# Linear attention with a gated feed-forward block: fewer turns of the identity at the start, one stored form of x sooner, and the last tile's sum added in PSUM

## The chip, the cores and the metric

The kernel runs on one core of one Trainium2 chip. The metric is the device time of one execution in microseconds. A core has a matrix engine (TensorE, PE in the profile), a vector engine (VectorE, DVE), a scalar engine (ScalarE, ACT), a general engine (GpSimd, POOL) and a queue engine (SyncE, SP), which issues nearly all transfers here. SBUF is the working memory and PSUM the memory that TensorE writes, in eight banks.

## The reference

All arrays are float32: x is 2048 by 576, `wqkv` 576 by 1728, `wo` 576 by 576, `w_gate` and `w_up` 576 by 4608, `w_down` 4608 by 576; there are 32 heads of 18.

```python
xn = layernorm(x)
q, k, v = split(xn @ wqkv)                 # per head
phi = lambda t: where(t > 0, t + 1, exp(t)) + 1e-6
kv  = einsum("sd,se->de", phi(k), v);  z = phi(k).sum(0)
s   = (phi(q) @ kv / (phi(q) @ z + 1e-6)) @ wo
h   = gelu(xn @ w_gate) * (xn @ w_up)
out = x + s * silu(h @ w_down)
```

## The kernel before, in words

Every large product is made of float32r words: an operand is cut into a high word (a ScalarE copy) and a low word (a VectorE subtraction), and several passes of TensorE add up their products in a PSUM bank. The rows of x are sixteen tiles of 128; four tiles make a block of 512 (`TBN`), and pairs of blocks make the two halves `s = 0, 1`. The columns of x are split in two halves j.

All instructions are pinned to the order in which the program writes them, on each engine (`keep_in_program_order`), so the listing is the schedule. `big(i, ...)`, `mid(i, ...)` name SBUF slots with one buffer each: a tile made in a slot waits until all users of the tile before it there are done. `bank` takes one of six PSUM banks in turn, `own_bank` one of two others.

**The start.** TensorE turns (transposes) a 128 by 128 identity into a bank that nobody reads, in the loop at L1230, while the first loads arrive. Then tile 0 of x is normalized (`spread`, `scales`, `center` on VectorE, with two small steps on ScalarE), transposed by `turn(0)` (L205), copied out by `save` on ScalarE, and multiplied by the raw weights (`x_mm_plain`). For the tiles after it, `turn`, `place` (the words of x, named xo_B), `save` and `x_mm` (L128, tile kv) repeat; the words of the weights are made by `kv_hi` on ScalarE and `kv_lo` on VectorE or GpSimd (tile wkv).

**Between the two halves.** After tile 7 the q products of blocks 0 and 1 run, five groups each, through `q_store(tb, gi)`: TensorE fills a bank, ScalarE and VectorE form phi of it (tiles e_q and ph), GpSimd adds the two, and SP stores the result. Group 4 is a group of mixed rows that are only transposed. The dictionary `behind` says what is written behind each group. `form(nm)` cuts one of four differences of blocks of x (T1, T3, T2, T4, made by `difference`) into words in slot 12 and stores it in DRAM: one copy of 1536 columns on ScalarE, two subtractions on VectorE, and one transfer on SP of 1280 KB (tile xo_T, stored as kept_T). Tiles 8 and 9 of x are prepared in the same stretch (`turn(N0)`, `place(N0)`, `center(N0 + 1)`, `spread(N0 + 2, 2)`), and then the kv tiles of the second half begin. `spread_sel` and what follows turn kv and q into s.

**The feed-forward block.** Gate and up run as products of block matrices with sums of blocks formed beforehand (`matrix`, L769), and h goes to DRAM in pieces (hs). The down product takes 26 products (`PROD`), each of nine K-tiles (`kt`), in four banks of 288 columns, one for each row tile j; `read` adds banks into the accumulators (`acc`). `UNITS` says which K-tiles go together: 0 to 3 in the first two units, 4 to 8 in the rest.

**The end.** In the last product `down_all` leaves the loop after the first two units, closes the output of the product before, and then runs K-tiles 4 to 8 tile by tile (j = 0 to 3). Behind each tile `close_last` adds the bank to the accumulator on VectorE and takes Silu on ScalarE; the multiplication with s, the addition of x and the store (`rest`) are written one tile later. The last tile does all this in two halves of 144 columns.

Of the kernel before, what the change touches and what calls it, by code (L numbers as in the profile page):

```python
# [11 lines left out]
AF = mybir.ActivationFunctionType  # L12
# [10 lines left out]
HALF = D // 2  # L23
# [3 lines left out]
TT = TBN // P  # L27
# [47 lines left out]
PROD = (  # L75
# [8 lines left out]
)  # L84
SIGN = (-1, 1, -1, -1, 1, -1, 1, 1)
# [5 lines left out]
def block_kernel(ctx, tc, x, xe, wq_d, wkv_d, wo, wgu_d, wd_d, out):  # L91
# [9 lines left out]
    def own_bank(name):  # L101
        return ps.tile([P, 512], F32, tag="own", bufs=2, name=name)

    def big(i, shape, dt, name):
        return sb.tile(shape, dt, tag=f"b{i}", bufs=1, name=name)
# [7 lines left out]
    def gl_tile(shape, name, dt=F32):  # L113
        return sb.tile(shape, dt, tag="gl", bufs=6, name=name)
# [6 lines left out]
    def act(*args, **kw):  # L121
        pin(nc.scalar.activation(*args, **kw))  # L122

    def vec(op, *args, **kw):
        pin(getattr(nc.vector, op)(*args, **kw))  # L125
# [7 lines left out]
    def dma(out, in_, eng=None):  # L133
        tc.keep_in_program_order((eng or nc.sync).dma_start(out=out, in_=in_))
# [42 lines left out]
    def scales(n0):  # L177

        n, mv, st = mom.pop(n0)
        v, r, c = (st[:, i, 0:n] for i in range(1, 4))  # L180
        if n == 1:
            vec("tensor_scalar", c, r, r, -0.5, op0=ALU.mult, op1=ALU.mult)
            vec("tensor_scalar", c, c, v, 1.5, op0=ALU.mult, op1=ALU.add)
            vec("tensor_scalar", c, c, r, None, op0=ALU.mult)
        else:
            vec("scalar_tensor_tensor", c, r, -0.5, r, op0=ALU.mult, op1=ALU.mult)
            vec("tensor_mul", c, c, v)
            vec("scalar_tensor_tensor", c, c, 1.5, r, op0=ALU.add, op1=ALU.mult)
        for t in range(n):
            scale_of[n0 + t] = mv[:, t, 0:1], c[:, t : t + 1]  # L190

    def center(n):

        xs = xstat[n // 2][:, n % 2]
        m, r = scale_of.pop(n)
        vec("tensor_scalar", xs, xs, m, r, op0=ALU.subtract, op1=ALU.mult)
# [258 lines left out]
    def q_mm(tb, gi, o):  # L455
        s, b = divmod(tb, 2)
        pq = bank(f"q_{tb}_{gi}")
        if gi == NHG - 1:
            t = qt.pop(tb)
            for i in range(TT):  # L460
                pin(nc.tensor.transpose(
                    pq[:, i * P : (i + 1) * P], t[:, i].rearrange("p r j -> p (r j)"), ident
                ))
        else:
            n = 0
            for j, nm in enumerate(BS[b]):
                for wi, xi, rows in PASSES:
                    mm(
                        pq, q_part(j, wi, slice(gi * P, (gi + 1) * P)), xo[s][nm][:, xi, :],
                        start=(n == 0), stop=(n == 2 * len(PASSES) - 1),  # L470
                    )
                    n += 1
        phi(o, pq, f"q{tb}_{gi}")

    def q_store(tb, gi):
        if tb not in ph_d:
            ph_d[tb] = dr.tile([P, NHG, TBN], F32, name=f"phd_{tb}")
        o = gl_tile([P, TBN], f"ph_{tb}_{gi}")
        q_mm(tb, gi, o)
        dma(out=ph_d[tb][:, gi, :], in_=o)  # L480
# [395 lines left out]
    def run_events(at):  # L876
        for f in events.pop(at, []):
            f()
# [54 lines left out]
    reg, acc_t, banks, raw_v, hi_v, word, early = {}, {}, {}, {}, {}, {}, {}  # L933

    def load_reg(at, nm, third=None):
        if at not in reg:
            b = big(REG[at], [P, REG_W], F32, f"b_{at}")
            reg[at] = b[:, 0 : KT * HALF].rearrange("p (k d) -> p k d", k=KT)
        j, c = int(nm[0]) - 1, int(nm[1]) - 1
        par, f = divmod(KP[j], 2)  # L940
        src = wd_d[par::2, :, f, c * HALF : (c + 1) * HALF].rearrange("g p d -> p g d")
        k = slice(0, KT) if third is None else slice(3 * third, 3 * third + 3)
        dma(out=reg[at][:, k], in_=src[:, k])
# [133 lines left out]
    def acc_of(o):  # L1077
        i, j = ACCS[o]
        if i not in acc_t:
            acc_t[i] = big(i, [P, 2, TT, HALF], F32, f"acc_{i}")  # L1080
        return acc_t[i][:, j]
# [19 lines left out]
    sxs = {}  # L1101

    def places(o):
        i, c = divmod(o, 2)
        tb = TP[i]
        cols = slice(c * HALF, (c + 1) * HALF)
        rows = lambda j: slice(tb * TBN + j * P, tb * TBN + (j + 1) * P)
        return tb, cols, rows
# [22 lines left out]
        vec("tensor_add", t[:, 0], t[:, 0], t[:, 1])  # L1131
        stores.append(lambda: dma(out=out[rows(j), cols], in_=t[:, 0]))

    def close_last(o, j, p, parts):

        _, cols, rows = places(o)
        w = HALF // parts
        y, t, b = acc_of(o)[:, j], sxs[o][j], banks[p % 2][j]
        d = dict(PROD[p][3])[o]
        cs = [slice(i * w, (i + 1) * w) for i in range(parts)]  # L1140
        for c in cs:
            vec("tensor_add" if d > 0 else "tensor_sub", y[:, c], y[:, c], b[:, c])
            act(y[:, c], y[:, c], AF.Silu, scale=float(SIGN[o]))

        def rest():
            for c in cs:
                z = t[:, 0, c]
                vec("tensor_mul", z, y[:, c], z)
                vec("tensor_add", z, z, t[:, 1, c])
                dma(  # L1150
                    out=out[rows(j), cols.start + c.start : cols.start + c.stop], in_=z
                )

        return [rest]

# [17 lines left out]
    def down_all():  # L1173
        late = []
        last = NP - 1
        for u in range(NP * NU):
            p, k = divmod(u, NU)
            n = KT * p + 2 * k
            for at in sorted(events):
                if at <= H_END + n // 2:  # L1180
                    run_events(at)
            if p in LOADS and k < 3:
                load_reg(*LOADS[p], k)
            if k == 0:
                for o, e in ENDS.items():
                    if e == p:
                        load_sx(o)
            if k < 2:
                change(p + 1, k)
                if p in SHARED:  # L1190
                    make_words(p + 1, k)
            elif k < 4:
                make_words(p + 1, k - 2)
                if p + 1 in SHARED and p:
                    make_words(p + 2, k - 2)
            cut(u + 2)
            if p == last and k == 2:
                break
            for kt in range(*UNITS[k]):
                down_mm(p, kt, range(TT))  # L1200
            load_unit(p + 1, k)
            run(stores)
            if k == 1 and p:
                read(p - 1)
                late += [
                    lambda o=o, j=j: close(o, j) for o, e in ENDS.items() if e == p - 1
                    for j in range(TT)
                ]
            else:
                run(late, 2)  # L1210
        run(late)
        run(stores)
        o = next(o for o, e in ENDS.items() if e == last)
        for j in range(TT):
            for kt in range(UNITS[2][0], KT):
                down_mm(last, kt, (j,))
            late += close_last(o, j, last, 2 if j == TT - 1 else 1)
            run(late, len(late) - 1)
        run(late)

# [6 lines left out]
        ins=[], outs=[], act_func_set_id=LN_EXP,  # L1227
    )))
    first = [own_bank(f"idle_{i}") for i in range(2)]
    for i in range(34):  # L1230
        pin(nc.tensor.transpose(first[i % 2][:, 0:P], ident, ident))  # L1231
    load_x(0, 1)
    load_kv(0, 0)
# [86 lines left out]
    for n in range(3, 2 * TT):  # L1320
# [3 lines left out]
        if n >= TT:  # L1324
            j, c = divmod(n - TT, 2)
# [16 lines left out]
    N0 = 2 * TT  # L1342

    def form(nm):
        keep(0, nm, build(0, nm, 12))

    behind = {
        (0, 0): [lambda: kv_mm(N0 - 1), lambda: spread(N0, 2), lambda: difference(0, 3)],
        (0, 1): [lambda: scales(N0), lambda: center(N0), lambda: q_store(1, 4)],
        (0, 2): [lambda: form("T1")],  # L1350
        (0, 3): [lambda: turn(N0), lambda: place(N0)],
        (1, 0): [lambda: form("T3"), lambda: save(N0)],
        (1, 1): [lambda: center(N0 + 1), lambda: spread(N0 + 2, 2), lambda: scales(N0 + 2)],
# [143 lines left out]
```

## Time and profile before

| | |
|---|---|
| median of 3 runs | 1473.43 us (1472.06 to 1473.94) |
| the profiled execution, its own time | 1472.68 us |
| its span | 1470.9 us |
| busy TensorE, VectorE, ScalarE, GpSimd | 1461.8, 1138.0, 572.0, 579.1 us |
| turns of the identity | 34, from 1.75 us to 8.05 us |
| end of TensorE, end of VectorE | about 1465.6 us, 1468.1 us |

In the rows, "out<-in" names the tile that is written and the tiles that are read, with buffer numbers left out. A row of the timeline begins with the start and the length in microseconds; several like instructions are merged ("x4"), and the bracket tells how long the engine was idle before it and what ended that. A line number can be that of a helper: L125 is every VectorE operation, L122 every ScalarE operation, L131 GpSimd's, L128 every plain matmul, L134 every transfer.

### The profile page before, as it was taken

The numbers are of one execution on the slowest core, as the hardware profiler recorded it, in microseconds if no ns is written. First come the engines' busy times: TensorE is split into PE (matmuls) and PEld (weight loads), VectorE is DVE, ScalarE is ACT, GpSimd is POOL, SyncE is SP. The second block draws the span as 40 slices with busy tenths as digits, with TensorE's granted clock in tenths as the row PEclk, the third lists the DMA queues.
The fourth block names the chain that finished last, engine by engine and source line by source line (L and its number), as shares of the span: only waits on it lengthen the run. The fifth ranks groups of instructions, "written<-read, shape, count | busy, mean of one in ns | idle before, by whom it ended". The sixth has DMA issues, their size and how long they took to land.

```text
span 1470.9 us, 21966 instructions
## 1 busy us (share of the span) xinstructions
PE 1461.8 (99%) x8184; PEld 1303.9 (89%) x8184; DVE 1138.0 (77%) x1581; ACT 572.0 (39%) x936; POOL 579.1 (39%) x513
## 2 busy tenths in 40 slices
PE   9999999999999999999999999999999999999998
PEld 8989989988888888888888888888889999999998
DVE  7566477466878788877778888778788978989888
ACT  5445355433222332223223223322335556455444
POOL 3332340125655667655674755757632000000000
PEclk9999999999999999999999999999999999999999
DMA  4435004442242323334153242423379888767886
GB/s 175 157 135 204 5 2 180 147 189 86 93 144 97 125 87 116 128 115 136 51 172 100 94 136 73 157 87 101 128 271 345 270 258 253 244 190 233 278 287 216
DMA packets 116148, 230.43 MB, mean 157 GB/s; under 512 B 10874, under 2 KB 44410, under 8 KB 113994
## 3 DMA queue, kind: packets, MB, share of 16 engines
q1 hardware_dynamic: 113386, 216.97, 44.0%
q0 software_dynamic: 2656, 12.06, 2.2%
q8 instruction: 65, 1.06, 0.3%
q14 instruction: 41, 0.34, 0.1%
HBM read 146.37 MB, written 82.58 MB: 156 GB/s over the span
## 4 chain that ended last, share of the span: by engine, by line
PE 96%; DVE 2%; issue 1%; DMA 0%; ACT 0%; POOL 0%; ACTq 0%; DVEq 0%; POOLq 0%
PE bd L128 23%; PE ga L769 16%; PE al L769 16%; PE de L769 16%; PE kv L128 8%; PE be L769 8%; PE s L128 4%; PE q L128 3%; PE kv_a L128 1%; PE xt L205 1%; DMA raw_h<-hs 0%; PE idle L1231 0%; PE d L128 0%; PE kw L128 0%; DVE acc L125 0%
## 5 line engine op out<-in xcount | busy, mean ns | idle before, releaser
L131 POOL TENSOR_TENSOR sm<-raw 128x384 f32<-128x384 f32 x72 | 75.2, 1044 | 152.0 <-DMA raw<-in_wgu_dram 107.4
L128 PE MATMUL kv<-wkv,xo_B 128*128 128x388 f32 (+2 forms) x658 | 127.9, 349 | 0.5 <-DVE xo_B L125 0.4
L128 PEld LDWEIGHTS kv<-wkv,xo_B 128*128 128x128 f32 x658 | 118.8, 188 | 2.4 <-DVE xo_B L125 0.7
L125 DVE TENSOR_TENSOR wa<-sm,wa 128x768 fp32r<-128x768 f32 x72 | 92.5, 1285 | 36.1 <-ACT wa L122 35.2
L128 PE MATMUL bd<-w_head,hi 128*128 128x288 f32 x516 | 118.0, 294 | 0.0
L125 DVE TENSOR_TENSOR wb<-raw,wb 128x256 fp32r<-128x256 f32 (+1 forms) x108 | 107.0, 991 | 7.3 <-ACT wb L122 5.8
L125 DVE TENSOR_TENSOR wa<-raw,wa 128x256 fp32r<-128x256 f32 x72 | 68.2, 947 | 50.7 <-ACT wa L122 49.6
L122 ACT ACTIVATE hi<-raw_h 128x1024 fp32r<-128x1024 f32 x59 | 62.4, 1059 | 90.0 <-PE bd L128 60.9
L128 PE MATMUL bd<-w_end,hi 128*128 128x288 f32 x448 | 89.8, 294 | 0.0
L122 ACT ACTIVATE spot_h<-spot_h 128x512 f32<-128x512 f32 x49 | 30.8, 633 | 151.4 <-DVE spot_h L125 151.4
L128 PEld LDWEIGHTS bd<-w_head,hi 128*128 128x128 f32 x516 | 87.0, 188 | 0.1
L125 DVE TENSOR_TENSOR raw_h<-raw_h,hi 128x1024 fp32r<-128x1024 f32 x59 | 71.9, 1223 | 16.7 <-ACT hi L122 16.7
L128 PE MATMUL bd<-w_end,raw_h 128*128 128x288 f32 x264 | 77.9, 295 | 0.0
L122 ACT ACTIVATE u<-al 128x512 f32<-128x512 f32 x72 | 41.0, 592 | 90.0 <-PE al L769 60.9
L122 ACT ACTIVATE wa<-sm 128x1152 fp32r<-128x1152 f32 x36 | 41.8, 1161 | 84.8 <-PE de L769 84.8
L128 PEld LDWEIGHTS bd<-w_end,hi 128*128 128x128 f32 x448 | 71.9, 188 | 0.0
L128 PE MATMUL bd<-beside,raw_h 128*128 128x288 f32 x240 | 70.9, 295 | 0.0
L131 POOL TENSOR_TENSOR spot_h<-spot_h,spot_h 128x512 f32<-128x512 f32 x45 | 62.3, 1390 | 2.9 <-DVE spot_h L125 2.4
L769 PE MATMUL ga<-xo_B,wb 128*128 128x512 f32 x252 | 63.0, 389 | 0.0
L769 PE MATMUL al<-xo_B,wa 128*128 128x512 f32 x252 | 63.0, 389 | 0.0
L769 PE MATMUL al<-xr_B,wb 128*128 128x512 f32 x252 | 63.0, 389 | 0.0
L769 PE MATMUL al<-xr_B,wa 128*128 128x512 f32 x252 | 63.0, 389 | 0.0
(261 smaller groups left out, 4066.5 us busy)
## 6 DMA issues: line engine op xcount, KB each, us to landing
raw_h<-hs SPq DMA_DIRECT2D x176, 256.0 KB
raw<-in_wgu_dram SPq DMA_DIRECT2D x36, 768.0 KB
hs<-spot_h SPq DMA_DIRECT2D x90, 256.0 KB
hs<-spot_g SPq DMA_DIRECT2D x80, 256.0 KB
b<-in_wd_dram SPq DMA_DIRECT2D x42, 432.0 KB
hs<-spot_m SPq DMA_DIRECT2D x38, 256.0 KB
raw_g<-hs SPq DMA_DIRECT2D x22, 256.0 KB
kept_T<-xo_T SPq DMA_DIRECT2D x4, 1280.0 KB
```

Source lines behind the costliest of these rows:

```text
L122: pin(nc.scalar.activation(*args, **kw))
L125: pin(getattr(nc.vector, op)(*args, **kw))
L128: pin(nc.tensor.matmul(*args, **kw))
L131: pin(getattr(nc.gpsimd, op)(*args, **kw))
L205: pin(nc.tensor.transpose(xts[n][j][:, k, :], xs[:, j, k * P : (k + 1) * P], ident))
L769: nc.tensor.matmul(o, w[0:rows, wi, :], xop[0:rows, xi, :], start=(start and n == 0), stop=(n == len(PASSES) - 1), skip_group_check=True,)
```

## The change

The loop at the start makes 28 turns for 34. `form("T1")` moves from behind q group 2 of block 0 to behind q group 1, ahead of `q_store(1, 4)`; so T1's ScalarE copy, its two VectorE subtractions and its store on SP now come before the phi and the stores of the mixed group and of q group 2. The order of TensorE's instructions is the same but for the six turns. For the last row tile, a new step `add_in` adds the accumulator into the PSUM bank on VectorE, ahead of the last five K-tiles; these K-tiles then add to it in the bank, Silu reads the bank itself with the sign folded into its scale, and the last tile is closed in one piece of 288 columns, with one store for two.

```diff
+    def add_in(o, j, p):
+
+        b = banks[p % 2][j][:, 0:HALF]
+        vec("tensor_add" if dict(PROD[p][3])[o] > 0 else "tensor_sub", b, b, acc_of(o)[:, j])
+
-    def close_last(o, j, p, parts):
+    def close_last(o, j, p, added):
...
-        for c in cs:
-            vec("tensor_add" if d > 0 else "tensor_sub", y[:, c], y[:, c], b[:, c])
-            act(y[:, c], y[:, c], AF.Silu, scale=float(SIGN[o]))
+        if added:
+            act(y, b, AF.Silu, scale=float(SIGN[o] * d))
+        else:
+            vec("tensor_add" if d > 0 else "tensor_sub", y, y, b)
+            act(y, y, AF.Silu, scale=float(SIGN[o]))
...
         o = next(o for o, e in ENDS.items() if e == last)
+        add_in(o, TT - 1, last)
         for j in range(TT):
             for kt in range(UNITS[2][0], KT):
                 down_mm(last, kt, (j,))
-            late += close_last(o, j, last, 2 if j == TT - 1 else 1)
+            late += close_last(o, j, last, j == TT - 1)
             run(late, len(late) - 1)
...
-    for i in range(34):
+    for i in range(28):
         pin(nc.tensor.transpose(first[i % 2][:, 0:P], ident, ident))
...
-        (0, 1): [lambda: scales(N0), lambda: center(N0), lambda: q_store(1, 4)],
-        (0, 2): [lambda: form("T1")],
+        (0, 1): [
+            lambda: scales(N0), lambda: center(N0), lambda: form("T1"), lambda: q_store(1, 4),
+        ],
```

More of the change, by code (lines that the diff above doesn't have):

```diff
@@ L1132, in close @@
         stores.append(lambda: dma(out=out[rows(j), cols], in_=t[:, 0]))
-    def close_last(o, j, p, parts):
+    def add_in(o, j, p):
+        b = banks[p % 2][j][:, 0:HALF]
+        vec("tensor_add" if dict(PROD[p][3])[o] > 0 else "tensor_sub", b, b, acc_of(o)[:, j])
+    def close_last(o, j, p, added):
         _, cols, rows = places(o)
-        w = HALF // parts
-        y, t, b = acc_of(o)[:, j], sxs[o][j], banks[p % 2][j]
+        y, t, b = acc_of(o)[:, j], sxs[o][j], banks[p % 2][j][:, 0:HALF]
         d = dict(PROD[p][3])[o]
-        cs = [slice(i * w, (i + 1) * w) for i in range(parts)]
-        for c in cs:
-            vec("tensor_add" if d > 0 else "tensor_sub", y[:, c], y[:, c], b[:, c])
-            act(y[:, c], y[:, c], AF.Silu, scale=float(SIGN[o]))
-        def rest():
[L1146 to L1152, printed above, removed]
+        if added:
[3 more added lines that the diff above has]
+            act(y, y, AF.Silu, scale=float(SIGN[o]))
+        def rest():
+            z = t[:, 0]
+            vec("tensor_mul", z, y, z)
+            vec("tensor_add", z, z, t[:, 1])
+            dma(out=out[rows(j), cols], in_=z)
         return [rest]
```

## The prediction

> **What bounds the kernel now.** I read the page first (busy shares, then the chain that ended last), then the waits of TensorE alone, and then the timeline around each of the three places that the change touches.
>
> ```profile
> span 1470.9 us, 21966 instructions
> ...
> PE 1461.8 (99%) x8184; PEld 1303.9 (89%) x8184; DVE 1138.0 (77%) x1581; ACT 572.0 (39%) x936; POOL 579.1 (39%) x513
> ...
> PE 96%; DVE 2%; issue 1%; DMA 0%; ACT 0%; POOL 0%; ACTq 0%; DVEq 0%; POOLq 0%
> ```
>
> TensorE (PE) bounds it. It is idle for 1470.9 - 1461.8 = 9.1 us in all, so nothing that leaves its own work alone can win more than that. The waits of TensorE (total, times, longest) say where the idle time before the tail lies:
>
> ```profile
> PE idle L1231 <- POOL ident masks.py:199: 1.8, 1, 1.8
> PE xt L205 <- issue: 0.5, 1, 0.5
> PE kv L128 <- DVE xo_B L125: 0.4, 1, 0.4
> ...
> PE xt L205 <- DVE x L125: 0.2, 1, 0.2
> ```
>
> Only the 0.4 and the 0.2 belong to the stage that the change re-orders. The other things it can reach are TensorE's own "work" on the identity at the start, and what comes after its last matmul. A microsecond taken from the head or from a wait of TensorE is a microsecond off the end, as long as TensorE stays the bound in between, which it is in 96% of the chain.
>
> **Part 1, 28 turns for 34.** The windows of the tile idle give their pace (columns: PE busy and count, weight loads busy and count):
>
> ```profile
> 1.75:6.50 4.75, 4.75 (x23) 4.75 (x23) 1.00 0.96 350
> 6.50:7.81 1.31, 1.31 (x13) 1.31 (x12) 1.00 0.98 395
> ```
>
> Twenty-two turns fit into the first 4.75 us (one of the 23 straddles the border): 0.216 us each. The last twelve take 1.31 us: 0.109 each. The pace doubles near 6.5 us, while the granted clock reads 1.00 throughout, so the records of the clock do not show this step and the pitch does. Six turns fewer are six of the fast kind, if the step comes at the same time: 6 x 0.109 = 0.65 us. Whether the first transposes of x can use that, and whether it gets through to the end, is read from the chain (start, length, piece) and from VectorE's rows:
>
> ```profile
> 1.75 6.30 PE idle L1231 x34
> 8.05 0.51 PE xt L205 x3
> ...
> 8.58 0.50 ACT xf_B L122
> ...
> 12.94 0.87 ACT xo_B L122 x2
> ...
> 15.01 1.99 POOL wkv L131
> ...
> 18.86 6.83 PE kv L128 x36
> ```
>
> ```profile
> 6.41 0.68 DVE L125 TENSOR_SCALAR x<-x,mv,st 128x768 f32<-128x768 f32 x1
> ...
> 10.58 0.68 DVE L125 TENSOR_SCALAR x<-x,mv,st 128x768 f32<-128x768 f32 x1
> 11.18 1.61 DVE L125 TENSOR_TENSOR wkv<-rw,wkv 128x832 fp32r<-128x832 f32 x2
> 13.46 1.51 DVE L125 TENSOR_TENSOR xo_B<-xt,xo_B 128x256 fp32r<-128x256 f32 x4 [0.67 <-ACT xo_B L122]
> ```
>
> Tile 0 of x is ready at 6.41 + 0.68 = 7.09, and TensorE comes to it only at 8.05, so up to 0.96 can be used; with 28 turns it comes at 7.40, still after x, and the turns still cover the wait. From there the chain hands the shift on: ScalarE's copy waits for the transposes, the plain matmuls for the copy, and the second turn needs tile 1 of x, ready at 11.26, well ahead of 12.58 - 0.65 = 11.93. ScalarE's xo_B and wkv, GpSimd's wkv and the matmuls at 18.86 follow one another. VectorE is the one that could hold it: it is free at 12.79 and waited 0.67 until 13.46, just more than the 0.65 asked for; behind that it follows ScalarE or its own work and moves along. I take 0.65. Bounds: 0 if the pace steps up so early that x is the later one in both kernels, and 6 x 0.216 = 1.3 if it steps up after the turns.
>
> The Trainium skill (TensorE: Matmul & The Clock Gate, "Part 1: The HAM clock gate") says why this length can vary: the clock opens after a busy window of some 3.4 us, the window runs free of the kernel's start, and the warm-up is a time and not a number of matmuls. By it, an estimate: the step falls between one and two windows after the first turn, between 5.2 and 8.6 us here, and the six turns are worth anything between 0 and 1.3 us. The one trace has the step at 6.5, inside that.
>
> **Part 2, the first transformed form (T1) a group of q sooner.** T1, T3 and T2 are cut into the same buffer (slot 12) and each is stored from it, so each waits for the store of the one before. Rows of the timeline, in order of time:
>
> ```profile
> 95.32 0.64 ACT L122 ACTIVATE e_q<-e_q 128x512 f32<-128x512 f32 x1
> ...
> 99.58 1.48 ACT L122 ACTIVATE xo_T<-xf_B 128x1536 fp32r<-128x1536 f32 x1
> ...
> 101.15 2.20 DVE L125 TENSOR_TENSOR xo_T<-xf_B,xo_T 128x1024 fp32r<-128x1024 f32 x2 [1.41 <-ACT xo_T L122]
> ...
> 103.41 0.32 SPq L134 DMA_DIRECT2D kept_T<-xo_T  x1
> ...
> 109.30 1.49 ACT L122 ACTIVATE xo_T<-xf_B 128x1536 fp32r<-128x1536 f32 x1 [2.57 <-DMA kept_T<-xo_T]
> ...
> 112.81 0.32 SPq L134 DMA_DIRECT2D kept_T<-xo_T  x1
> ...
> 118.77 1.48 ACT L122 ACTIVATE xo_T<-xf_B 128x1536 fp32r<-128x1536 f32 x1
> ...
> 123.95 1.51 DVE L125 TENSOR_TENSOR xo_B<-xt,xo_B 128x256 fp32r<-128x256 f32 x4
> ...
> 124.43 2.15 PE L128 MATMUL kv<-wkv,xo_B 128*128 128x416 f32 x10 [0.37 <-DVE xo_B L125]
> ...
> 126.08 0.68 DVE L125 TENSOR_SCALAR x<-x,mv,st 128x768 f32<-128x768 f32 x1
> ...
> 126.82 0.87 PE L205 MATMUL xt<-ident,x 128*128 128x128 f32 x6 [0.24 <-DVE x L125]
> ```
>
> A store takes 109.30 - 103.41 = 5.9 us until ScalarE may go on. After the change T1's ScalarE cut follows the exponential of q group 1, ending 95.96, and runs to 97.4; VectorE's subtractions follow the centring and take 2.20, to about 100.4; the store goes out at 100.4 instead of 103.41, 3.0 us sooner. T3 can then start at 106.3 instead of 109.30; ScalarE has a group's phi in front of it, so I say 106.9. T3's store goes out at about 110.4 and lands at 116.3; T2 starts at 116.4 instead of 118.77, 2.4 us sooner. Behind T2 stand the things that TensorE waits for: xo_B of tile 9 on ScalarE and VectorE (123.95) and the centring of tile 10 (126.08). They come some 2.4 us sooner, and the two waits need only 0.37 and 0.24. Both go: 0.61 us.
>
> What the move delays: on ScalarE and VectorE the phi of the group of mixed rows and of q group 2 wait behind T1, by some 2.2 us; GpSimd's additions to them follow, and on SP T1's store now stands in front of those two phi stores. TensorE needs their PSUM banks only six allocations later, at the groups that it starts at about 105 and 108, when they have been read since about 101.5. ScalarE's phi of q group 3 can slip by 2 us behind GpSimd's addition, which would cost T3 0.2. None of it reaches TensorE, so nothing is charged. Bounds: 0.61, all that TensorE waits there, and 0 if the waits only move on to the next tile.
>
> **Part 3, the last sum.** VectorE's last row of work, TensorE's row for the last tile, and the transfers (window, last two columns DMA share and GB/s):
>
> ```profile
> 1462.29 0.81 DVE L125 TENSOR_TENSOR acc<-acc,bd 128x288 f32<-128x288 f32 x2
> ...
> 1463.42 0.29 PE L128 MATMUL bd<-beside,hi 128*128 128x288 f32 x1
> ...
> 1464.97 0.46 DVE L125 TENSOR_TENSOR sx<-sx 128x288 f32<-128x288 f32 x1
> ...
> 1465.60 0.52 DVE L125 TENSOR_TENSOR acc<-acc,bd 128x144 f32<-128x144 f32 x2 [0.17 <-PE bd L128]
> ...
> 1466.04 0.45 DVE L125 TENSOR_TENSOR sx<-acc,sx 128x288 f32<-128x288 f32 x1
> 1466.52 0.46 DVE L125 TENSOR_TENSOR sx<-sx 128x288 f32<-128x288 f32 x1
> 1466.90 0.30 DVE L125 TENSOR_TENSOR sx<-acc,sx 128x144 f32<-128x144 f32 x1
> ...
> 1467.80 0.31 DVE L125 TENSOR_TENSOR sx<-sx 128x144 f32<-128x144 f32 x1
> ```
>
> ```profile
> 1467.80:1468.40 0.60, 0.00 (x0) 0.00 (x0) 0.30 (x1) 0.00 (x0) 0.00 (x0) 0.50 0.69 246
> 1468.40:1469.40 1.00, 0.00 (x0) 0.00 (x0) 0.00 (x0) 0.00 (x0) 0.00 (x0) 0.50 0.49 148
> ```
>
> Today VectorE stands before 1465.60 until TensorE has ended, with the multiply and the addition of tile 2 queued behind it, and then has eight instructions left, ending at 1468.11. After: the new addition into PSUM runs at 1462.29, before the two of that row, and pushes what follows by 0.36 (the pitch of that row: 0.81 - 0.45). The wait goes; tile 2's multiply follows the row at 1464.97 directly: 1464.97 + 0.36 + 0.38 = 1465.7, tile 3's a pair later (1466.90 - 1466.04 = 0.86) at 1466.6, its addition ends about 1467.5. ScalarE's Silu reads the bank when TensorE ends, about 1465.6; the copy out of PSUM at 8.58 took 0.50 for 384 columns, so 288 end by 1466.1, before 1466.6: VectorE's queue, no longer TensorE, sets it. That is 0.57 sooner. The store is now one of 288 columns, not the second of two halves: tile 2's, of that size, had its last bytes 1468.40 - 1466.98 = 1.4 us after its addition (1466.52 + 0.46), the half 1469.40 - 1468.11 = 1.3. So 0.1 goes back; I take 0.44, between 0 and 0.6.
>
> The new wait: TensorE's tile 3 needs the addition, done at 1462.74, and starts at 1463.42. The cover is 0.68 us; without it each microsecond is one at the end, and nothing but tile 3's fifteen matmuls is queued there.
>
> **Sum.** 0.65 + 0.61 + 0.44 = 1.70 us. The profiled execution took 1472.68 us, 1.78 around its span; it gives 1470.98. It lies 0.75 below the median of the three runs, 1473.43, to which the measured time answers: 1473.43 - 1.70 = 1471.7.
>
> **The rivals.**
> - The pace steps up early and x is late anyway: part 1 is worth nothing, 1.05 stays, 1472.4. For it: x is only 0.31 earlier than the new end of the turns. Against: this trace. 0.10.
> - The pace steps up late: 1.3 for part 1, 2.35 in all, 1471.1. 0.12.
> - The two waits of part 2 only move on, and the change does not do there what it says: 1.09, 1472.3. Against: 2.4 us of lead for 0.61. 0.08.
> - The new addition comes late and TensorE waits in front of tile 3: it decides from 0.68 us of delay of VectorE, which has eight instructions waiting for loads and Silus before it; at 1.5 us late part 3 is a loss of 0.4 and the time 1472.6. 0.07.
> - Slower: fewer turns are too little to lift the pace. They then all run at 0.216, 28 x 0.216 = 6.05, and end where they end now; part 1 is gone, and the matmuls after them run at half pace for as long as the first stretch lasted, 4.75 us, which loses 2.4. Net 1.05 - 2.4: 1.3 slower, 1474.8; two such stretches 1477.1. It decides if a gap such as the one before the plain matmuls falls where the turns used to be. Against: the pace rose near 6.5, before the new end at 7.4. 0.08.
> - The forecast: 0.55, alone 1470.4 to 1473.0.
>
> **How the numbers follow.** The three runs before lie between 1472.06 and 1473.94, and a measurement of this kernel can tell about 0.2%, 2.9 us, from no change. Faster by more than that, below 1470.5, needs the late step and a kind scatter: 0.07 from the forecast, 0.06 from the second rival, 0.13. Slower by more needs the two slow stretches, or a longer wait than priced: 0.06. The rest, 0.81, is within it. The range takes in the first four rivals and the scatter of the runs: 1470.2 to 1473.9.
>
> **What would show it.** Right: idle ends near 7.4 and transposes of x begin there; the matmuls now at 18.86 begin near 18.2; T1's store is issued near 99.8 and T2's cut starts near 115.7 (both less 0.65); neither wait of 0.37 and 0.24 is left; VectorE's last addition ends some 1.9 us after TensorE instead of 2.5. Wrong: turns at 0.216 to their end, a wait of kv or xt of like size a tile later, a wait of bd for VectorE before the last fifteen matmuls, or a last store that takes longer than 1.4 us.

## The result, and the profile after

| | before | after |
|---|---|---|
| median | 1472.54 us (1471.28 to 1473.94, 19 runs) | 1470.32 us (1469.58 to 1471.74, 19 runs) |
| the profiled execution, its span | 1472.68, 1470.9 us | 1470.93, 1468.6 us |

The ratio is 0.9985, with a 95% interval of 0.9979 to 0.9992: 2.2 us less, 0.15%. Forecast were 1.7 us less, and no change larger than 0.2%.

The page of the kernel after, the same lines as before:

```profile
span 1468.6 us, 21945 instructions
...
PE 1459.7 (99%) x8178; PEld 1302.2 (89%) x8178; DVE 1134.3 (77%) x1578; ACT 571.9 (39%) x935; POOL 579.0 (39%) x513
...
PE 95%; DVE 2%; issue 1%; ACT 1%; DMA 1%; POOL 0%; SPq 0%; DVEq 0%; ACTq 0%; POOLq 0%
```

TensorE still bounds it. Its busy time fell by 2.1 us, 1.7 of it in the turns (4.62 us, by the windows below, for 6.30). The waits of TensorE after (total, times, longest), without the one before the first turn (1.8) and one of 0.2 in tile b, which both kernels have:

```profile
PE xt L205 <- PE idle L1234: 1.0, 1, 1.0
PE xt L205 <- issue: 0.6, 1, 0.6
PE kv L128 <- ACT xf_B L122: 0.3, 1, 0.3
PE ga L769 <- DVE u L125: 0.2, 1, 0.2
```

The 0.4 for xo_B and the 0.2 for x are gone, as forecast. New is the first row: 1.0 us in which TensorE has no turns left and x is not there yet. It carries the name of the turns, but it ends when x comes, as the next rows show.

**The start.** The turns by windows (PE busy and count, then weight loads), the head of the chain of waits, and VectorE's row for tile 0 of x, all after:

```profile
1.75:4.25 2.50, 2.50 (x12) 2.50 (x13) 1.00 0.91 307
4.25:4.75 0.50, 0.50 (x5) 0.50 (x4) 1.00 1.09 449
4.75:6.50 1.75, 1.62 (x15) 1.38 (x13) 1.00 1.01 402
```

```profile
1.75 4.63 PE idle L1234 x28
6.38 0.97 issue
7.36 0.53 PE xt L205 x3
...
8.46 3.45 PE kv L128 x8
...
18.20 6.82 PE kv L128 x36
```

```profile
6.58 0.68 DVE L125 TENSOR_SCALAR x<-x,mv,st 128x768 f32<-128x768 f32 x1
```

The pace rose at about 4.4 us, not at 6.5: 2.50/12 = 0.21 us a turn before it, 1.62/15 = 0.11 behind it. The turns ended at 6.38, a microsecond ahead of the forecast; x was ready at 6.58 + 0.68 = 7.26 and the transposes began at 7.36. The 36 matmuls at 18.86 now begin at 18.20, 0.66 sooner.

**The transformed forms.** Rows picked from the timeline after: ScalarE's cuts of T1, T3, T2 and the stores of the first two, then tile 9's words, tile 10's centring, and TensorE's rows beside them:

```profile
95.27 1.47 ACT L122 ACTIVATE xo_T<-xf_B 128x1536 fp32r<-128x1536 f32 x1
99.58 0.32 SPq L134 DMA_DIRECT2D kept_T<-xo_T  x1
106.03 1.48 ACT L122 ACTIVATE xo_T<-xf_B 128x1536 fp32r<-128x1536 f32 x1
109.53 0.32 SPq L134 DMA_DIRECT2D kept_T<-xo_T  x1
115.50 1.47 ACT L122 ACTIVATE xo_T<-xf_B 128x1536 fp32r<-128x1536 f32 x1
117.33 8.00 PE L128 MATMUL kv<-wkv,xo_B 128*128 128x412 f32 x42
120.67 1.51 DVE L125 TENSOR_TENSOR xo_B<-xt,xo_B 128x256 fp32r<-128x256 f32 x4
122.80 0.68 DVE L125 TENSOR_SCALAR x<-x,mv,st 128x768 f32<-128x768 f32 x1
125.17 0.82 PE L205 MATMUL xt<-ident,x 128*128 128x128 f32 x6
```

T3's cut no longer waits for T1's store (no bracket at 106.03). Tile 10 of x is ready at 123.48, 1.7 us ahead of its transposes at 125.17. TensorE goes through its 42 matmuls without a gap: 125.17 - 117.33 = 7.84 us. The row of before that answers to it:

```profile
117.94 6.13 PE L128 MATMUL kv<-wkv,xo_B 128*128 128x412 f32 x32
```

There the same stretch takes 126.82 - 117.94 = 8.88. I call this length T below; the move made it 1.04 us shorter, not 0.61.

**The end.** Rows picked from the timeline after: the addition into the bank, tile 3's first and last matmul, Silu out of the bank, and VectorE's last two; then the last matmul of before.

```profile
1460.40 0.46 DVE L125 TENSOR_TENSOR bd<-bd,acc 128x288 f32<-128x288 f32 x1
1461.74 0.29 PE L128 MATMUL bd<-beside,hi 128*128 128x288 f32 x1
1463.59 0.29 PE L128 MATMUL bd<-w_end,raw_g 128*128 128x288 f32 x1
1463.92 0.41 ACT L122 ACTIVATE acc<-bd 128x288 f32<-128x288 f32 x1 [0.41 <-PE bd L128]
1464.67 0.45 DVE L125 TENSOR_TENSOR sx<-acc,sx 128x288 f32<-128x288 f32 x1
1465.16 0.46 DVE L125 TENSOR_TENSOR sx<-sx 128x288 f32<-128x288 f32 x1
```

```profile
1465.27 0.29 PE L128 MATMUL bd<-w_end,raw_g 128*128 128x288 f32 x1
```

VectorE ends 1465.62 - 1463.88 = 1.74 us after TensorE, where it took 1468.11 - 1465.56 = 2.55. From TensorE's end to the end of the span it is 4.72, and was 5.34: 0.62 less.

So the span's 2.3 us are 0.66 + 1.04 + 0.62. Between these places the gate and up stage is 0.5 longer in this pair and the down stage 0.5 shorter, in code that the change does not touch.

### The profile page after: what moved, and what is told of

It reads as the page before. It is cut to its first block, busy times and chain, and to the rows that moved or that the text cites. A ratio compares the mean times of both kernels' runs of the same rounds, so it can differ in the third digit from the quotient of the medians.

```text
span 1468.6 us, 21945 instructions
## 1 busy us (share of the span) xinstructions
PE 1459.7 (99%) x8178; PEld 1302.2 (89%) x8178; DVE 1134.3 (77%) x1578; ACT 571.9 (39%) x935; POOL 579.0 (39%) x513
## 4 chain that ended last, share of the span: by engine, by line
PE 95%; DVE 2%; issue 1%; ACT 1%; DMA 1%; POOL 0%; SPq 0%; DVEq 0%; ACTq 0%; POOLq 0%
PE bd L128 24%; PE ga L769 15%; PE de L769 15%; PE al L769 15%; PE kv L128 8%; PE be L769 8%; PE s L128 4%; PE q L128 3%; PE kv_a L128 1%; PE xt L205 1%; DVE sx L125 1%; DMA hs<-spot_h 1%; DVE wb L125 0%; PE d L128 0%; PE kw L128 0%
## 5 line engine op out<-in xcount | busy, mean ns | idle before, releaser
L769 PE MATMUL ga<-xr_B,wb 128*128 128x512 f32 x252 | 63.0, 389 | 0.0
```

The source lines that it names most:

```text
L769: nc.tensor.matmul(o, w[0:rows, wi, :], xop[0:rows, xi, :], start=(start and n == 0), stop=(n == len(PASSES) - 1), skip_group_check=True,)
```

## The experiments

Kernels 1 to 3 hold one part of the change each, kernels 4 to 6 all but one part; five more push one step past its edge or try to win more. One table for all, worked out from each kernel's profiled execution as above: the length of the turns and the start of the first transposes of x, the start of the 36 matmuls, T, T1's store (from its issue to T3's cut, where the cut waits for it), the down stage (from its first matmul, near 1091 us, to TensorE's end), and from TensorE's end to VectorE's end and to the end of the span.

| kernel | turns, x | 36 kv | T | store | down | tail | median us (range, runs) |
|---|---|---|---|---|---|---|---|
| before | 6.30, 8.00 | 18.86 | 8.88 | 5.89 | 373.1 | 2.55, 5.34 | 1472.54 |
| after | 4.62, 7.36 | 18.20 | 7.84 | | 372.6 | 1.74, 4.72 | 1470.32 |
| 1 turns alone | 6.01, 7.72 | 18.58 | 8.12 | 5.12 | 372.3 | 2.54, 5.34 | 1471.18 (1470.23 to 1472.76, 11) |
| 2 T1 alone | 6.54, 8.24 | 19.11 | 7.84 | | 373.1 | 2.54, 5.36 | 1470.87 (1469.97 to 1471.84, 11) |
| 3 sum alone | 6.22, 7.92 | 18.78 | 9.05 | 6.05 | 372.3 | 1.73, 4.72 | 1472.17 (1471.28 to 1473.96, 11) |
| 4 all but the turns | 6.74, 8.44 | 19.31 | 7.84 | | 372.7 | 2.02, 4.93 | 1470.64 (1469.26 to 1471.68, 11) |
| 5 all but T1 | 6.24, 7.83 | 18.96 | 8.16 | 5.17 | 373.2 | 1.97, 4.93 | 1471.63 (1469.72 to 1473.95, 11) |
| 6 all but the sum | 5.73, 7.43 | 18.30 | 7.84 | | 373.5 | 2.54, 5.30 | 1471.04 (1470.19 to 1473.58, 11) |
| 7 24 turns | 4.71, 7.31 | 18.14 | 7.84 | | 372.4 | 1.75, 4.66 | 1470.43 (1469.64 to 1471.66, 11) |
| 8 12 turns | 2.82, 7.33 | 19.73 | 7.84 | | 373.5 | 1.76, 4.73 | 1472.26 (1470.89 to 1473.75, 10) |
| 9 addition late | 4.88, 7.33 | 18.16 | 7.84 | | 374.8 | 1.44, 4.39 | 1473.22 (1471.81 to 1474.60, 10) |
| 10 two on GpSimd | 4.93, 7.22 | 18.10 | 7.84 | | 372.3 | 1.76, 4.74 | 1470.56 (1469.39 to 1471.73, 11) |
| 11 one on GpSimd | 5.34, 7.25 | 18.10 | 7.84 | | 372.6 | 1.90, 4.85 | 1470.94 (1469.73 to 1471.62, 11) |

The kernel before, run beside them, had medians of 1472.15 to 1472.49. The runs of one kernel scatter by 2 to 4 us, so a part worth less than 1 us is read from the profiles first and from the medians second.

**1, turns alone** (before, with 28 turns).

```diff
-    for i in range(34):
+    for i in range(28):
```

> The kernel before with 28 turns for 34 and nothing else. Theory A (the six turns are worth what the pace at that moment makes of them, and nothing where the pace has risen early): over many runs between 0.3 and 0.8 us faster than before, and in the profile the first transposes of x start at the later of two times, end of the turns or tile 0 of x ready (about 7.1 to 7.3). Rival B (always six fast turns, 0.65 us, whenever the pace rises): the turns end 0.65 us sooner than 34 would in the same execution and the transposes follow them directly. Rival C (fewer turns leave TensorE at half pace): turns at 0.216 us to their end, plain matmuls of 416 columns at twice their length, 1.3 us slower or more.

Measured: 1471.18, ratio 0.9991 (0.9982 to 1.0000), 1.3 us less, more than the 0.3 to 0.8 of Theory A; the transposes begin at 7.72 and the 36 matmuls 0.28 sooner than in before. The span of this execution is 1.7 shorter, and most of that is not the turns: the down stage is 0.8 shorter, and T is 8.12, 0.76 less, although nothing of part 2 is in this kernel. The rows for T:

```profile
103.20 0.32 SPq L134 DMA_DIRECT2D kept_T<-xo_T  x1
108.32 1.49 ACT L122 ACTIVATE xo_T<-xf_B 128x1536 fp32r<-128x1536 f32 x1 [1.81 <-DMA kept_T<-xo_T]
117.71 7.99 PE L128 MATMUL kv<-wkv,xo_B 128*128 128x412 f32 x42
125.83 0.87 PE L205 MATMUL xt<-ident,x 128*128 128x128 f32 x6
```

The same store took 108.32 - 103.20 = 5.12 us in place of 5.89, and most of the stall went with it. Part 2 is not worth a fixed sum.

**2, T1 alone** (before, with the moved `form`).

```diff
-        (0, 1): [lambda: scales(N0), lambda: center(N0), lambda: q_store(1, 4)],
-        (0, 2): [lambda: form("T1")],
+        (0, 1): [
+            lambda: scales(N0), lambda: center(N0), lambda: form("T1"), lambda: q_store(1, 4),
+        ],
```

> The kernel before with only T1 moved a group sooner. Theory A (each wait of TensorE costs more than its idle row says, since the row begins where the last matmul's pipelined length ends): the stretch from the first kv matmul of tile 8's second part to the transposes of tile 10 falls from 8.88 us to about 7.84, and the time by 1.0 us. Rival B (the idle rows 0.37 and 0.24 are the whole): 0.6 us, and the other 0.4 that the changed kernel gained between 118 and 126 us comes from its other edits. Rival C (the waits move on): a wait of kv or xt of like size a tile later, 0 to 0.3 us.

Measured: 1470.87, ratio 0.9989 (0.9980 to 0.9998), 1.6 us less than before beside it, 0.6 more than Theory A's 1.0 and within the interval; T is 7.84, as Theory A had it.

**3, sum alone** (before, with `add_in` and the new `close_last`, as in the diff of the change).

> The kernel before with only the last tile's sum added in PSUM and its single store. Theory A: VectorE ends about 1.75 us after TensorE's last matmul instead of 2.5, the single store gives back 0.1 to 0.2, and the time falls by 0.6 us; no wait of TensorE for VectorE in the last fifteen matmuls. Rival B (0.44 as summed in the prediction, the rest of the changed kernel's gain being a chance shift of VectorE's queue against TensorE): 0.4 to 0.5 us, VectorE ending 1.95 us after TensorE.

Measured: the tail is 1.73 and 4.72, as in after. The time, 1472.17, ratio 1.0000 (0.9991 to 1.0009), shows little of Theory A's 0.6: 0.3 us by the medians. By itself that is inconclusive; kernel 6 was run for it.

**4, all but the turns** (after, with 34).

```diff
-    for i in range(28):
+    for i in range(34):
```

> The changed kernel with 34 turns again, so only the turns undone. Theory A (the six turns are worth the six at the pace of the moment, less where tile 0 of x is later; the nine traces so far have the pace rising between 4.4 and 7.2 us, which makes 0 to 0.7 us of it): 0.3 to 0.7 us above the changed kernel's 1470.3, and in the trace the transposes of x directly behind the turns, between 7.4 and 8.4 us. Rival (the turns are worth the 1.3 us that the run with the turns alone was faster than before): 1471.6.

Measured: 1470.64, ratio to before 0.9989 (0.9980 to 0.9998). It is 0.3 us above after by the medians, 0.7 if each is taken from the before that ran beside it. The transposes begin at 8.44, directly behind the turns.

**5, all but T1** (after, with `form("T1")` back behind group 2).

```diff
-            lambda: scales(N0), lambda: center(N0), lambda: form("T1"), lambda: q_store(1, 4),
+            lambda: scales(N0), lambda: center(N0), lambda: q_store(1, 4),
...
+        (0, 2): [lambda: form("T1")],
```

> The changed kernel with T1 back behind q group 2, so turns and sum changed alone. Theory A (the stall that T1's move takes away is as long as the store of T1 makes it, 5.1 to 6.1 us in the traces so far, which gives 0.3 to 1.2 us): 0.8 to 1.2 us above the changed kernel, 1471.1 to 1471.5, with the stretch from the kv matmuls of tile 8's second part to the transposes of tile 10 between 8.1 and 9.1 us for 7.84, the longer the longer T1's store. Rival (the 1.6 us that the run with T1 alone was faster is the move's worth): 1471.9 or more.

Measured: 1471.63, ratio 0.9992 (0.9983 to 1.0001), 1.3 us above after; here too with a short store in the profile:

```profile
103.57 0.32 SPq L134 DMA_DIRECT2D kept_T<-xo_T  x1
108.74 1.49 ACT L122 ACTIVATE xo_T<-xf_B 128x1536 fp32r<-128x1536 f32 x1 [1.86 <-DMA kept_T<-xo_T]
118.09 7.99 PE L128 MATMUL kv<-wkv,xo_B 128*128 128x412 f32 x42
126.25 0.87 PE L205 MATMUL xt<-ident,x 128*128 128x128 f32 x6 [0.17 <-DVE x L125]
```

Four executions now have T1 in its old place: stores of 5.12, 5.17, 5.89 and 6.05 us give T of 8.12, 8.16, 8.88 and 9.05. T is 3.0 us more than the store in each. Nine with T1 moved give 7.84 each. So the stall is what the store takes beyond 4.84 us: 0.3 to 1.2 us in these.

**6, all but the sum** (after, with the `close_last` of before).

```diff
-        add_in(o, TT - 1, last)
...
-            late += close_last(o, j, last, j == TT - 1)
+            late += close_last(o, j, last, 2 if j == TT - 1 else 1)
```

> The changed kernel with the last tile's sum and stores as before, so turns and T1 changed alone. Theory A (the sum in PSUM is worth the 0.62 us by which the span ends nearer to TensorE's last matmul in both traces that have it, and its run alone, 0.3 us in the median, fell short by scatter): about 0.6 us above the changed kernel, near 1470.9, and 5.3 us from TensorE's end to the end of the span. Rival (its gain is no more than the 0.1 to 0.3 of the run alone): 1470.3 to 1470.6.

Measured: 1471.04, ratio 0.9991 (0.9982 to 1.0000), 0.7 us above after; the tail is 2.54 and 5.30 again. The down stage of this execution is 0.9 longer than after's, with a wait of its own among the waits of TensorE:

```profile
PE bd L128 <- DVE raw_h L125: 0.7, 1, 0.7
```

Rows of this kind, of 0.2 to 0.7, come in the executions of before and of kernels 2, 5 and 6, one of 0.9 (for raw_a) comes in kernel 8, and there is none in after and the other kernels. They belong to no part of the change, and are one source of the scatter.

**7, 24 turns** (after, with four fewer still).

> The changed kernel with 24 turns for 28. Theory A: where the pace rises late, 24 turns at 0.216 us end at 6.9 us, before tile 0 of x is ready near 7.2, so x and no longer the turns sets the start in every execution: 0 to 0.5 us faster than the changed kernel (0.2 in the middle), with the slow executions of the changed kernel (1471.3 to 1471.7) gone. Rival C (too few turns to lift the pace): in some executions the transposes and the plain matmuls run at half pace and the time is 1 us or more above the changed kernel's.

Measured: 1470.43, ratio 0.9986 (0.9977 to 0.9995), level with after. TensorE waits 0.8 us for x and the transposes begin at 7.31: once the turns end ahead of x, fewer of them win nothing. The longer executions, which Theory A wanted gone, are still there (1471.30 and 1471.66), so late turns are not what makes them long.

**8, 12 turns** (after, with sixteen fewer).

```diff
-    for i in range(28):
+    for i in range(12):
```

> The changed kernel with 12 turns for 28. Theory A (the pace rises after a stretch of busy TensorE, 2.9 to 6 us after the first turn in the executions seen so far): the turns end at 1.75 + 12 x 0.216 = 4.4 us, TensorE then stands idle for 2.9 us until tile 0 of x, so the pace rises only behind the plain matmuls or later; transposes and plain matmuls of 416 columns at about half pace, the matmuls that now begin at 18.2 begin 1 to 3 us later, and the time 1 to 3 us above the changed kernel's 1470.3. Rival (the pace follows time since the start and not the work): full pace from about 6 us on, nothing lost, 1470.0 to 1470.4.

Measured: 1472.26, 1.9 us above after. TensorE's timeline, and under it the first six transposes of before:

```profile
1.75 2.82 PE L1234 MATMUL idle<-ident 128*128 128x128 f32 x12 [1.75 <-POOL ident masks.py:199]
7.33 1.51 PE L205 MATMUL xt<-ident,x 128*128 128x128 f32 x6 [2.76 <-issue]
8.79 4.66 PE L128 MATMUL kv<-rw,xf_B 128*128 128x416 f32 x8
```

```profile
8.00 0.88 PE L205 MATMUL xt<-ident,x 128*128 128x128 f32 x6
```

The twelve turns are all of the slow kind (2.82/12 = 0.23). TensorE then stands 2.76 us; x comes no later than elsewhere, but six transposes take 1.51 us where before had 0.88, and the eight plain matmuls 4.66 where the chain after has 3.45. The 36 matmuls begin at 19.73 for 18.20. This is the rival "fewer turns are too little", made to happen. The pace rises only near 11 us, where the twelve executions with 24 turns or more have it by 7.7, so it does not simply follow the time since the start.

**9, the addition late** (after, with `add_in` just ahead of the last tile's K-tiles).

```diff
-        add_in(o, TT - 1, last)
         for j in range(TT):
+            if j == TT - 1:
+                add_in(o, j, last)
```

> The changed kernel with the addition into PSUM written just ahead of the last tile's five K-tiles, so behind the sums, the closings of tiles 0 and 1 and the sum of tile 2 on VectorE; nothing is left out. Theory A (the new wait costs nothing only because VectorE does it early): the sum of tile 2 waits for TensorE's tile 2, tile 1's closing (0.86) and the addition (0.46) follow, and TensorE waits 1.5 to 1.9 us in front of its last fifteen matmuls; all of it shows in the end, 1.2 to 1.9 us above the changed kernel's 1470.3. Rival (the wait is hidden by work that TensorE has queued): no wait of bd for VectorE, the same time within 0.3.

Measured: 1473.22, ratio 1.0005 (0.9996 to 1.0014), 2.9 us above after. Its wait and the rows around it:

```profile
PE bd L128 <- DVE bd L125: 2.1, 1, 2.1
```

```profile
1462.95 0.46 DVE L125 TENSOR_TENSOR bd<-bd,acc 128x288 f32<-128x288 f32 x1
1463.46 0.40 PE L128 MATMUL bd<-beside,hi 128*128 128x288 f32 x1 [2.06 <-DVE bd L125]
1466.19 0.46 DVE L125 TENSOR_TENSOR sx<-acc,sx 128x288 f32<-128x288 f32 x1 [1.94 <-ACT acc L122]
```

TensorE stands 2.06 us in front of tile 3, and the shorter tail (4.39 for 4.72) gives 0.33 back: 1.7 net, as Theory A had it, and the profiled span is 1.5 longer than after's. By the medians it is 2.9; what the other 1.2 is, beside scatter, stays open.

**10 and 11, x added on GpSimd** for tiles 0 and 1, or for tile 0 alone, to shorten VectorE's queue at the end.

```diff
-            vec("tensor_add", z, z, t[:, 1])
+            (pool if j < 2 else vec)("tensor_add", z, z, t[:, 1])
```

> The changed kernel with the addition of x for tiles 0 and 1 of the last output on GpSimd, which is idle there, for VectorE. Theory A (at the end VectorE's queue is the bound, not TensorE): VectorE's last addition ends 1.4 to 1.5 us after TensorE's last matmul, set by the Silu of the last tile, for 1.74, and the time falls by 0.2 to 0.35 against the changed kernel. Rival (GpSimd and VectorE get in each other's way, or the last store is the bound): the end stays at 1.7 us or more behind TensorE, no gain.

> The changed kernel with the addition of x on GpSimd for tile 0 of the last output alone, so that GpSimd has ended before VectorE's last three operations. Theory A (VectorE's queue is the bound at the end, and with two tiles on GpSimd it was the overlap of the two engines that gave the gain back): VectorE's last addition ends 1.44 us after TensorE's last matmul, as in the run with the late addition, 4.4 us from there to the end of the span for 4.72, 0.3 us in the time, within the scatter of the runs. Rival (VectorE's multiplies of tiles 0 and 1 are lengthened by GpSimd just as much): 1.7 us again.

Measured: 1470.56 and 1470.94, ratios 0.9986 and 0.9989; nothing gained over after, and VectorE ends 1.76 and 1.90 us behind TensorE, as both rivals had it. Rows of kernel 10, then of kernel 11:

```profile
1461.41 0.81 POOL L131 TENSOR_TENSOR sx<-sx 128x288 f32<-128x288 f32 x1 [326.37 <-DVE sx L125]
1461.55 1.35 DVE L125 TENSOR_TENSOR sx<-acc,sx 128x288 f32<-128x288 f32 x2
1462.60 0.94 POOL L131 TENSOR_TENSOR sx<-sx 128x288 f32<-128x288 f32 x1 [0.39 <-DVE sx L125]
1462.93 0.93 DVE L125 TENSOR_TENSOR sx<-sx 128x288 f32<-128x288 f32 x1
```

```profile
1461.71 0.81 POOL L131 TENSOR_TENSOR sx<-sx 128x288 f32<-128x288 f32 x1 [327.74 <-DVE sx L125]
1461.86 0.98 DVE L125 TENSOR_TENSOR sx<-acc,sx 128x288 f32<-128x288 f32 x1
```

VectorE's addition beside GpSimd's takes 0.93 us, and its multiply 0.98, where after has 0.46 and 0.45. What was taken off VectorE's queue came back as slower instructions on it. The Trainium skill (SBUF — State Buffer, "Who interferes with whom") says that a VectorE instruction with two SBUF inputs and a GpSimd instruction that reads SBUF contend. The rows agree.

No kernel tried is measurably faster than the changed one.

## Why the prediction was right, and where only its sizes were off

Forecast were 1471.7 (1470.2 to 1473.9) from three runs with a median of 1473.43; the before measured beside the changed kernel has 1472.54, the changed kernel 1470.32. That is 1.4 below the forecast and only 0.1 inside the range, and below 1470.5, to which the prediction gave a chance of 0.13. Of the 1.4, 0.9 is the median of the three runs, which happened to lie above that of the nineteen; 0.5 is the sizes of the parts. The difference was 2.2 us against the forecast's 1.70, in the three places named and, as far as the profiles show, in no other.

**Part 1, 0.65: the size fits this pair of profiles (0.66) by another course, so by luck.** The forecast had the pace rising at 6.5 and the turns ending at 7.40, behind x. In after it rose near 4.4, the turns ended a microsecond before that, and x set the start. That is the course of the first rival; its conclusion, that the part is then worth nothing, does not hold against the before that was profiled, which had the late step. It would against a before with the same early step: 1.75 + 12.4 x 0.216 + 21.6 x 0.109 = 6.8, about 7.0 with the length of the last turn, also ahead of x. From the turns' length in the other profiles with 24 turns or more, a rise between 4.4 and 7.7 us follows; in kernel 5 all 28 turns ran at the slow pace (6.24/28 = 0.22), and the transposes behind them at the full one. So the step moves from one execution to the next. The upper bound of 1.3 would need a step behind 34 slow turns, at 1.75 + 34 x 0.216 = 9.1 us; none came so late with the turns still running.

Over the profiles the start of the transposes is 8.15 on average with 34 turns (four) and 7.45 with 28 (seven), 0.7 apart, but the four all had a step behind 6.3. If each of the twelve steps seen is applied to both numbers of turns, with x at 7.3 us, the six turns are worth 0 to 0.7, and 0.4 on average, by estimate. The medians give 0.3 or 0.7 (kernel 4) and 1.3 (kernel 1), and their intervals do not tell these apart; the part's mean is not measured closer than that.

One reading in the prediction was wrong: that the records of the clock do not show the step. The windows print 1.00 from the start, but the list of clock changes in each packed trace, which the views do not print, begins with full clock only 0.1 to 0.2 us behind the step: at 6.65 us in before, 4.55 in after, 7.86 in kernel 5; in kernel 8 it begins at 11.26. The 1.00 ahead of that is no measurement. The stretches of full clock last 1457.49, 1460.90 or 1464.32 us in the thirteen traces, which is 427, 428 and 429 times 3.413 us. That fits a clock that changes on a grid of this pitch, with the kernel beginning at another place on it in each execution; no run sets that place, so this much is argued and not shown.

The Trainium skill (TensorE: Matmul & The Clock Gate, "Part 1: The HAM clock gate") let me estimate a rise between 5.2 and 8.6 us. That it varies holds; 4.4 us in after is 2.65 us behind the first turn, less than the one full window of 3.4 that I took as its floor.

**Part 2, 0.61: mechanism right, size too small.** The rows came where forecast: T3's cut at 106.03 (106.9 less 0.65), T2's at 115.50 (115.7), and no wait a tile later; that rival is out. The term that was mis-sized is "the two waits, 0.37 and 0.24". A wait in these rows begins only when the matmul before it has ended, and matmuls overlap: T of 7.84 is 42 matmuls at 0.187, but one lasts some 0.35. The first one behind the wait of 0.37 also lasts 0.46, 0.11 longer. In before 32 of them from 117.94 would let the next begin at 123.9, and it began at 124.43; ten more from there would end at 126.3, and the transposes began at 126.82. That is 0.5 lost at each, 1.04 in all. Second, I took one length of T1's store as given; kernels 1, 3 and 5 show the stall following it from 0.3 to 1.2 us.

**Part 3, 0.44: mechanism right, 0.62 measured.** The forecast's 1.95 us from TensorE's end to VectorE's end were 1.74: the addition began 3.48 us ahead of TensorE's end, where the row that it replaces stood 3.27 ahead. VectorE's queue was 0.2 earlier than in the profile I counted from, and it, not TensorE, sets this end, as forecast. Where the queue was later, in kernels 4, 5 and 11, the tail is 1.90 to 2.02 and 4.85 to 4.93, close to the forecast (1.90 is kernel 11, which GpSimd delayed); without the edit it is 5.30 to 5.36. The larger store gave back 0.2 (2.98 us from VectorE's end to the span's, for 2.79), not 0.1. Silu out of the bank took 0.41 and ended at 1464.33, before VectorE came to tile 3 at 1464.67. The addition was done at 1460.86, 0.88 ahead of tile 3's first matmul; kernel 9 shows the cost without that cover, a wait of 2.06 us of which 1.7 reach the end, nearly the microsecond for microsecond of the rival.

Leaving out one part costs 0.3 (turns), 1.3 (T1) and 0.7 us (sum) by the medians, 2.3 together, against 2.2 measured for all. Alone they are worth 1.3, 1.6 and 0.3, 3.2 together. With intervals of about 1.3 us to each side the times alone do not rank the parts; their sizes rest on the profiles.

## What to carry to other kernels

Price a stall of TensorE from the pitch of its matmuls and the start of the next one, not from the idle row: here rows of 0.61 us stood for 1.04. Where a wait ends on a transfer or on a pace that moves from one execution to the next, a removed wait is worth a range, and one profile shows one point of it. When edits are each smaller than the scatter of the runs, leave them out one at a time and read the place of each in the profile; the medians alone put the same part at 0.3 and at 1.3.

## What the runs showed of the hardware

- The pace of TensorE at the start doubled between 2.65 and about 6 us after the first turn, in the executions with 24 turns or more. There the first record of the clock begins 0.1 to 0.2 us behind the step (4.55 to 7.86 us); in all thirteen traces full clock lasted 427 to 429 times 3.413 us. After twelve turns and 2.76 us of standing, the next matmuls were still slow (1.51 us for six transposes, for 0.88).
- One store of 1280 KB took 5.12 to 6.05 us from its issue until ScalarE could write its buffer again.
- VectorE's addition into a PSUM bank took 0.46 us for 288 columns beside running matmuls, as much as one in SBUF.
- VectorE's instructions with two SBUF inputs went from 0.45 to 0.98 us beside an addition on GpSimd.
